# Nine head pairs alone instead of twelve, and one batch's first chunk beside the next three

## The chip, the cores and the metric

The kernel runs on one core of one Trainium2 chip. The metric is the device time of one launch in microseconds (us). Three runs of the kernel before gave 1332.28, 1333.82 and 1337.2 us, median 1333.82.

## What is computed

Attention over 4 batches, 12 heads, 448 positions and a head width of 64, with q and k normed by their root mean square, and then two dense layers without a residual:

```python
q_n, k_n = rmsnorm(q, g_q), rmsnorm(k, g_k)          # over the 64 of a head
attn = softmax(q_n @ k_n.T / 8);  x = attn @ v       # (4, 12, 448, 64)
x = x.transpose(0, 2, 1, 3).reshape(1792, 768)
h = x @ w_in;   x = (s * relu(h)**2 + b) @ w_out     # layer 1: 768 -> 2048 -> 768
h = x @ w2_in;  out = (h * cos(h)) @ w2_out          # layer 2, the same sizes
```

All is float32; the weights reach the device as 64-bit floats.

## The kernel before, in words

**Pairs.** Attention goes through 24 pairs of heads, six to a batch, numbered here 0 to 23 in that order; names in the trace carry batch and pair of the batch, so pair 8 is `1_2`. A pair is done in four chunks of 112 queries. A chunk is two score products on TensorE (PE, `sc`, line 193), two row maxima on VectorE (DVE, `top`, line 205), two exponentials on ScalarE (ACT, `pr`, line 208), and two chunks later eight transposes (`tp`, line 226) copied out by ACT and DVE (`pT`). Once a pair: squares (ACT, line 135), their sums (DVE, `ss`, line 141), the norms (ACT and GpSimd (POOL), lines 150 to 162), the transposes of q and k (`pt_q`, `pt_k`, line 173, copied out as `qT` and `kT`), the product with v (`av`, line 249) and its scaling (DVE, `xf`, line 257). The score product of a chunk also waits for the exponentials of two chunks earlier (line 197).

**Layers.** A layer's 2048 hidden columns go in 8 chunks of two column tiles. Each product is three passes of split operands (high by high, low by high, high by low). An *in* unit (line 400, 18 matmuls) makes one hidden tile for one batch, an *out* unit (line 452, or 479 in layer 2) adds a chunk to the result; in layer 1 an out unit is 6 matmuls.

**Weights.** A weight tile comes in two halves. A half of raw weight is a DMA, two ACT passes (lines 371, 372), three DVE passes (375 to 377), a store to DRAM in layer 1 (line 380), an ACT cast (338) and a subtraction on POOL (339). A half that was stored before is a DMA, the cast and a subtraction on DVE. Three weight tiles are held.

**Order.** All pairs of batches 0 and 1 (12) run alone. Then layer 1 of these two batches runs, chunk after chunk, beside the 12 pairs of batches 2 and 3, whose results go to DRAM. They are reloaded (`reload`, line 512; `xr`, then the split `xh` and `xl`) for layer 1 of batches 2 and 3, and layer 2 follows for all four. The units stand in one list; after each unit, `steps` is drawn on as far as a cost account allows (line 588), and a scheduler then sets the order on each engine from readiness. `ALONE` counts the batches whose pairs run alone and take their PSUM banks for `pt`, `rt` and `av` from the pool that the layers use later (line 165); other pairs take them from the two `tp` banks. The first six raw halves are held back behind chosen exponentials (line 374), the first weight DMA behind the score product of step `START` (line 364).

Of the kernel before, what the change touches and what calls it, by code (L numbers as in the profile page):

```python
# [33 lines left out]
def body(ctx, tc, q, k, v, g_q, g_k, w1_in, w1_out, s_in, b_in, w2_in, w2_out, out):  # L34
    nc = tc.nc
    B, H, S, D = q.shape
# [3 lines left out]
    NCH = 4  # L40
# [8 lines left out]
    NT = 2 * S // P  # L49
    SKEW = 2  # L50
    LAG_T = 2
    START, GATE = 10, 33
    ALONE = 2
    PAIR = 12.1
    LOOK = 8

# [54 lines left out]
    def attention(keep):  # L111
# [3 lines left out]
        tail = {}  # L115

        def line(engine, first, last=None):
            if engine in tail and (engine == "PE" or len(exps) <= NCH * NP * ALONE):
                issue_after(first, tail[engine])
            tail[engine] = last or first  # L120
            return first
# [40 lines left out]
                    rs[:, n].unsqueeze(3).to_broadcast([CP, 2, NCH, D]), ALU.mult)  # L162

        def bank(i, name):
            if pairs[i][0] < ALONE:
                return psm.tile([P, 512], F32, tag="mo", name=name, bufs=2)
            return ps.tile([P, 512], F32, tag="tp", name=name)

# [93 lines left out]
        def emit(f, i, *a):  # L262
            if 0 <= i < len(pairs):
                f(i, *a)
# [13 lines left out]
        squares(1)  # L278
        means(1)
        norms(1)  # L280
        for s in range(n + 5):
            i, r = divmod(s, NCH)
            old = i - 1 if 0 < i <= len(pairs) else None
            alone = old is not None and pairs[old][0] < ALONE
            cost = 0.0
            if r == 1:
                emit(load, i, "v")
                emit(load, i + 3, "qk")
                emit(flip, i + 1, "q")
                cost += 0.46  # L290
            if r == 2:
                emit(flip, i + 1, "k")
                cost += 0.46
            if s < n:
                scores(s)
                cost += 0.93
            if r == 1:
                emit(unflip, i + 1, "q")
            if r == 2:
                emit(unflip, i + 1, "k")  # L300
            if r == 3 and old is not None and not alone:
                finish(old)
            if LAG_T <= s < n + LAG_T:
                turn(s - LAG_T)
                cost += 0.9
            if r == 0:
                if 0 <= i - 2 < len(pairs) and pairs[i - 2][0] < ALONE:
# [12 lines left out]
            if i == 0 and r < 3:  # L320
                for part in ((), (squares,), (means, norms))[r]:
                    emit(part, 2)
            else:
                if r == 0:
                    emit(means, i + 2)
                if r == 1:
                    emit(norms, i + 2)
                if r == 3:
                    emit(squares, i + 3)
            yield cost  # L330


# [8 lines left out]
    def load_weight(key):  # L341
        layer, seg, kind, a, e = key
        w = ((w1_in, w1_out), (w2_in, w2_out))[layer][kind]
        name = "_".join(map(str, key))
        wh = wp.tile([P, 2 * CW], F32R, tag="wh", name=f"wh_{name}", bufs=3)
        wl = wp.tile([P, 2 * CW], F32R, tag="wl", name=f"wl_{name}", bufs=3)
        weights[key] = wh, wl
        for o in range(2):
            kk = f"{name}_{o}"
            hi_part, lo_part = (z[:, o * CW:(o + 1) * CW] for z in (wh, wl))  # L350
            if (layer, kind, a, e, o) in plain:
                t = wp.tile([P, CW], F32, tag="t", name=f"t_{kk}", bufs=3)
                nc.sync.dma_start(t, plain[layer, kind, a, e, o])
                halves(t, hi_part, lo_part, nc.vector)
                continue
            own = "xb" in pools or count["raw"] % 3 < 2
            raw = (wp if own else pools["att"]).tile([P, CW], I64, tag="raw", name=f"raw_{kk}", bufs=2 if own else 1)
            count["raw"] += 1
            if kind == 0:
                src = w[o * CW:(o + 1) * CW, a * P:(a + 1) * P].rearrange("(c p) f -> p c f", p=P)  # L360
                dma = nc.sync.dma_start(raw.rearrange("p (c f) -> p c f", f=P), src)
            else:
                dma = nc.sync.dma_start(raw, w[(CF * a + o) * P:(CF * a + o + 1) * P, e * CW:(e + 1) * CW])
            if seg == 0 and kind == 0 and a == 0:
                follow(dma, marks["start"])
            ru = raw.bitcast(U32).rearrange("p (n two) -> p n two", two=2)
            lo, hi = ru[:, :, 0], ru[:, :, 1]
            c = wp.tile([P, CW], U32, tag="c", name=f"c_{kk}", bufs=2)
            cf = c.bitcast(F32)
            t = wp.tile([P, CW], U32, tag="t", name=f"t_{kk}", bufs=3)  # L370
            for z in (nc.scalar.activation(cf, hi.bitcast(F32), AF.Copy, scale=2.0**-112),  # L371
                      nc.scalar.activation(t, lo, AF.Copy, scale=LSCALE, bias=-0.5)):
                if count["raw"] <= 6:
                    issue_after(z, exps[GATE + 2 * (count["raw"] - 1)])
            nc.vector.scalar_tensor_tensor(t, hi, 0x80000000, t, ALU.bitwise_and, ALU.bitwise_or)  # L375
            nc.vector.tensor_scalar(cf, cf, VMAX, -VMAX, ALU.min, ALU.max)
# [137 lines left out]
        nc.sync.dma_start(t, stash[layer, b, c])  # L514
        xs.setdefault((layer, b), []).append(split(t, pool, f"{layer + 1}_{b}_{c}", nc.vector if c % 4 < 2 else nc.gpsimd))

    segs = [(0, (0, 1), range(NCK)), (0, (2, 3), range(NCK)), (1, (0, 1, 2, 3), range(NCK))]
    units = []
    chunks = [(seg, ck) for seg, (_, _, r) in enumerate(segs) for ck in r]
    ins = [[("in", segs[seg][0], seg, ck, f, b) for f in range(CF) for b in segs[seg][1]] for seg, ck in chunks]  # L520
# [1 line left out]
    for seg, ck in chunks:  # L522
# [6 lines left out]
    for n in range(len(chunks)):  # L529
        if chunks[n][0] < 2 and chunks[n + 1][0] != chunks[n][0]:  # L530
            ins[n].sort(key=lambda u: (u[5], u[4]))
    for n, (seg, ck) in enumerate(chunks):
        units += ins[n][SKEW if n else 0:]
        if n + 1 < len(chunks):
            if chunks[n + 1][0] != seg:
                units.append(("next", seg + 1))
            early = ins[n + 1][:SKEW]
        else:
            early = []
        units += early + outs[n]  # L540

    def weight_of(u):
        kind, layer, seg, ck, a, b = u
# [16 lines left out]
        while finished["pairs"] < batches * NP:  # L560
            next(steps)

    until(ALONE)
    last = {max(n for n, u in enumerate(units) if u[:3] == ("in", 0, 0) and u[5] == b): b + ALONE for b in range(ALONE)}
    rate = 1.05 * PAIR * NP * (B - ALONE) / sum(3.39 if u[0] == "in" else 1.13 for u in units[:min(last)])
    debt = 0.0
    seg = 0
    again = []
    for n, u in enumerate(units):
        ahead(n + LOOK)  # L570
        if u[0] == "next":
            seg = u[1]
            if seg == 1:
                for _ in steps:
                    pass
                att_scope.close()
                pools["xb"] = ctx.enter_context(tc.tile_pool(name="xb", bufs=2 * NE))
                pools["mb"] = ctx.enter_context(tc.tile_pool(name="mb", bufs=2))
                pools["psb"] = ctx.enter_context(tc.tile_pool(name="psb", bufs=2, space=PSUM))
                again = [(1, b, c, pools["xb"]) for b in range(2) for c in range(NE)]  # L580
            continue
        if seg == 1 and again and n % 4 == 0:
            reload(*again.pop(0))
        if seg > 1:
            while again:
                reload(*again.pop(0))
        for cost in (unit_in if u[0] == "in" else unit_out)(*u[1:]):
            debt += cost * rate
            while debt > 0:
                c = next(steps, None)  # L590
                if c is None:
                    break
                debt -= c
        if n in last:
            until(last[n] + 1)
            for c in range(NP):
                reload(0, last[n], c, xa)


_INS = ['q', 'k', 'v', 'g_q', 'g_k', 'moe_w_in', 'moe_w_out', 'moe_s', 'moe_b', 'moe2_w_in', 'moe2_w_out']  # L600
# [25 lines left out]
```

## Time and profile before

| | |
|---|---|
| median of three runs | 1333.82 us |
| the profiled execution, its span | 1332.04 us, 1330.3 us |
| mean granted clock of TensorE | 0.986 |
| PE, DVE, ACT, POOL busy | 95%, 63%, 56%, 42% of the span |
| HBM traffic | 82 GB/s |

Stages, by what PE does: pairs alone to 204 us, layer 1 of batches 0 and 1 beside pairs 12 to 23 to about 546 us, layer 1 alone to about 850 us, layer 2 to the end. Busy PE is not PE at its peak: matmuls overlap, so one that is busy for 0.37 us follows the one before after about 0.20 us.

### The profile page before, as it was taken

Reading aid. Unit: us, or ns where it says so; the run is one execution under the profiler, and the core shown is the slowest. Engines: PE = TensorE matmul, PEld = TensorE weight load, DVE = VectorE, ACT = ScalarE, POOL = GpSimd, SP = SyncE. Lnnn points to the kernel's source line nnn. Section 1 sums busy time; section 2 is a strip of 40 time slices with the busy share of each in tenths; the row PEclk is TensorE's granted clock in tenths of the full one; section 3 lists DMA queues with packets and bytes.
Section 4 is the critical chain, followed back from the end, with each engine's and each line's share of the span. In section 5 each row is a group of like instructions: output and inputs, shape, how many; then the busy total and the mean of one; then the engine's idle time right before and its main releaser. Section 6 shows DMA issues by size and latency. Waiting matters only on the chain.

```text
span 1330.3 us, 18663 instructions
## 1 busy us (share of the span) xinstructions
PE 1261.0 (95%) x6624; PEld 1041.2 (78%) x6624; DVE 837.6 (63%) x1444; ACT 750.2 (56%) x1686; POOL 563.5 (42%) x624
## 2 busy tenths in 40 slices
PE   5999889999998999989999999989999999999998
PEld 2444437676776776878999999879999999999997
DVE  5666855568667676565444445754667677666655
ACT  5777856665555555444522223587756666566641
POOL 2334536453543423444422223454635544444531
PEclk9999979999999999999999999989999999999999
DMA  3212522433433333345311112211112122111105
GB/s 95 79 50 60 153 87 87 133 100 110 125 100 109 99 115 98 101 146 188 101 56 60 48 57 69 69 51 48 48 48 57 56 63 65 48 48 49 48 13 166
DMA packets 80382, 109.75 MB, mean 83 GB/s; under 512 B 7072, under 2 KB 70304, under 8 KB 80288
## 3 DMA queue, kind: packets, MB, share of 16 engines
q1 hardware_dynamic: 80288, 108.56, 27.4%
q8 instruction: 52, 0.85, 0.3%
q14 instruction: 42, 0.34, 0.1%
HBM read 84.94 MB, written 23.59 MB: 82 GB/s over the span
## 4 chain that ended last, share of the span: by engine, by line
PE 60%; DVE 14%; ACT 10%; DMA 7%; POOL 5%; issue 4%; SPq 0%; ACTq 0%; POOLq 0%; DVEq 0%
PE ph L400 23%; PE po L479 15%; PE po L452 12%; PE av L249 4%; PE sc L193 3%; ACT pr L208 3%; DMA raw<-in_moe_w_in_dram 3%; DVE t L375 3%; DMA raw<-in_moe_w_out_dram 3%; DVE top L205 2%; PE tp L226 2%; DVE ss L141 2%; ACT c L371 1%; DVE gt L415 1%; POOL wl L339 1%
## 5 line engine op out<-in xcount | busy, mean ns | idle before, releaser
L400 PE MATMUL ph<-xh,wh 128*128 128x448 f32 x768 | 281.2, 371 | 5.0 <-ACT hs L418 4.3
L400 PE MATMUL ph<-xl,wh 128*128 128x448 f32 x768 | 282.9, 369 | 0.9 <-POOL xl L98 0.5
L400 PE MATMUL ph<-xh,wl 128*128 128x448 f32 x768 | 283.4, 370 | 0.2 <-DVE wl L339 0.2
L430 POOL TENSOR_TENSOR gl<-gt,gh 128x448 fp32r<-128x448 f32 x128 | 156.1, 1225 | 177.8 <-ACT gh L429 177.6
L339 POOL TENSOR_TENSOR wl<-t,wh 128x384 fp32r<-128x384 f32 x128 | 138.0, 1097 | 98.8 <-ACT wh L338 80.7
L208 ACT ACTIVATE pr<-sc,top 112x448 f32<-112x448 f32 x192 | 120.5, 631 | 84.9 <-DVE top L205 84.8
L400 PEld LDWEIGHTS ph<-xh,wh 128*128 128x128 f32 x768 | 145.0, 189 | 19.8 <-ACT hs L418 5.0
L452 PE MATMUL po<-gh,wh 128*128 128x448 f32 x384 | 146.6, 383 | 12.3 <-DVE acc L461 7.2
L400 PEld LDWEIGHTS ph<-xl,wh 128*128 128x128 f32 x768 | 144.9, 189 | 15.2 <-issue 2.7
L400 PEld LDWEIGHTS ph<-xh,wl 128*128 128x128 f32 x768 | 145.1, 189 | 12.8 <-issue 2.0
L479 PE MATMUL po<-wh,gh 128*128 128x384 f32 x448 | 151.1, 338 | 2.7 <-DVE acc L487 1.5
L479 PE MATMUL po<-wh,gl 128*128 128x384 f32 x448 | 149.8, 334 | 0.0
L479 PE MATMUL po<-wl,gh 128*128 128x384 f32 x448 | 149.1, 334 | 0.0
L205 DVE TENSOR_REDUCE top<-sc 112x1 f32<-112x448 f32 x192 | 112.1, 618 | 57.1 <-PE sc L193 57.0
L461 DVE TENSOR_TENSOR acc<-po,acc 128x448 f32<-128x448 f32 x168 | 102.5, 619 | 69.2 <-PE po L452 68.7
L226 PEld LDWEIGHTS tp<-ident,pr 112*112 112x112 f32 x768 | 79.6, 136 | 82.3 <-DVE pT L230 21.5
L452 PE MATMUL po<-gh,wl 128*128 128x448 f32 x384 | 142.5, 371 | 1.1 <-POOL wl L339 1.1
L452 PE MATMUL po<-gl,wh 128*128 128x448 f32 x384 | 142.1, 371 | 0.0
L371 ACT ACTIVATE c<-raw 128x384 f32<-128x384 f32 x128 | 71.2, 556 | 119.8 <-DMA raw<-in_moe_w_out_dram 50.3
L487 DVE TENSOR_TENSOR acc<-po,acc 128x384 f32<-128x384 f32 x196 | 105.4, 551 | 50.7 <-PE po L479 50.5
L338 ACT CAST wh<-t 128x384 fp32r<-128x384 f32 x192 | 90.4, 512 | 83.0 <-PE po L452 45.3
L428 POOL TENSOR_TENSOR gt<-hs,gt 128x448 f32<-128x448 f32 x64 | 78.5, 1227 | 122.0 <-ACT gt L427 116.8
(82 smaller groups left out, 2241.4 us busy)
## 6 DMA issues: line engine op xcount, KB each, us to landing
raw<-in_moe_w_in_dram SPq DMA_DIRECT2D x64, 384.0 KB, 3.6
raw<-in_moe_w_out_dram SPq DMA_DIRECT2D x64, 384.0 KB, 3.4
wd<-t SPq DMA_DIRECT2D x64, 192.0 KB, 3.8
t<-wd SPq DMA_DIRECT2D x64, 192.0 KB, 2.4
rawq<-in_q_dram SPq DMA_DIRECT2D x24, 224.0 KB, 2.6
rawk<-in_k_dram SPq DMA_DIRECT2D x24, 224.0 KB, 3.0
rawv<-in_v_dram SPq DMA_DIRECT2D x24, 224.0 KB, 3.2
xd<-xf SPq DMA_DIRECT2D x12, 224.0 KB, 3.4
```

The lines of the kernel that those rows point to most:

```text
L205: line("DVE", nc.vector.tensor_reduce(tops[j], sc[j], axis=AX.X, op=ALU.max, negate=True))
L208: e = line("ACT", nc.scalar.activation(pr, sc[j], AF.Exp, bias=tops[j], scale=1.0, accum_out=st[i]["sums"][:, c, j:j + 1]))
L226: mm = [nc.tensor.transpose(tp[:, kc * CP:(kc + 1) * CP], pr[:, kc * CP:(kc + 1) * CP], ident[:CP, :CP]) for kc in range(NCH)]
L338: nc.scalar.copy(wh, w)
L339: eng.tensor_tensor(wl, w, wh.bitcast(F32), ALU.subtract)
L371: for z in (nc.scalar.activation(cf, hi.bitcast(F32), AF.Copy, scale=2.0**-112), nc.scalar.activation(t, lo, AF.Copy, scale=LSCALE, bias=- ...
L400: nc.tensor.matmul(h, a, m, start=(c == 0 and n == 0), stop=(c == NE - 1 and n == 2))
L430: nc.gpsimd.tensor_tensor(gl, gt, gh.bitcast(F32), ALU.subtract)
L452: marks["out"] = nc.tensor.matmul(po, a, m, start=(f == 0 and n == 0), stop=(f == CF - 1 and n == 2))
L461: nc.vector.tensor_tensor(at, po, at, ALU.add)
L479: nc.tensor.matmul(po, a, m, start=(f == 0 and n == 0), stop=(f == CF - 1 and n == 2))
L487: nc.vector.tensor_tensor(at, po, at, ALU.add)
```

## The change

- `ALONE` becomes a count of pairs, 9. Pairs 9 to 23 take the `tp` banks.
- Layer 1 gets five segments in place of two: chunk 0 for batch 0 alone, chunks 1 to 7 for batches 0 and 1, chunk 0 for batch 1 alone, then batches 2 and 3. The weights of chunk 0 are therefore loaded once more: 4 tiles, 8 stored halves.
- Segment 0 stands beside pairs 9 to 11, chunks 1 to 7 beside pairs 12 to 23, each with a rate of its own. Before chunk 1 the pairs of batch 1 are drawn to their end.
- `START` is 5 instead of 10; the six held raw halves wait for every fourth exponential from 12 on instead of every second from 33 on.
- The squares of a pair are emitted at step 2, their sums at step 3, the norms at the next step 0 (before: 3, next 0, next 1). The load of q and k comes after the sums.
- Reloads go out one after each unit, not six at once. The first in units of the next segment are sorted by batch; at the change to layer 2, four in units for batches 0 and 1 stand between the last twelve out units, three after each.

```diff
-    START, GATE = 10, 33
-    ALONE = 2
+    START, GATE = 5, 12
+    ALONE = 9
...
         def bank(i, name):
-            if pairs[i][0] < ALONE:
+            if i < ALONE:
                 return psm.tile([P, 512], F32, tag="mo", name=name, bufs=2)
...
+        load(3, "qk")
         for s in range(n + 5):
...
-                emit(load, i + 3, "qk")
...
-            else:
-                if r == 0:
-                    emit(means, i + 2)
-                if r == 1:
-                    emit(norms, i + 2)
-                if r == 3:
-                    emit(squares, i + 3)
...
+            if r == 0 and i > 0:
+                emit(norms, i + 2)
+            if r == 2:
+                emit(squares, i + 3)
+            if r == 3:
+                emit(means, i + 3)
+                emit(load, i + 4, "qk")
...
-                    issue_after(z, exps[GATE + 2 * (count["raw"] - 1)])
+                    issue_after(z, exps[GATE + 4 * (count["raw"] - 1)])
...
-    segs = [(0, (0, 1), range(NCK)), (0, (2, 3), range(NCK)), (1, (0, 1, 2, 3), range(NCK))]
+    segs = [(0, (0,), [0]), (0, (0, 1), range(1, NCK)), (0, (1,), [0]), (0, (2, 3), range(NCK)), (1, (0, 1, 2, 3), range(NCK))]
+    L2 = 4
...
+        ins[n + 1].sort(key=lambda u: (u[5] // 2, u[4], u[5]) if u[1] else (u[5], u[4]))
...
+            if given == 4:
+                for z in range(4):
+                    units += [ins[n + 1][z]] + outs[n][3 * z:3 * z + 3]
+            elif given:
+                units += ins[n + 1][:given] + outs[n]
...
-    rate = 1.05 * PAIR * NP * (B - ALONE) / sum(3.39 if u[0] == "in" else 1.13 for u in units[:min(last)])
+    rates = [1.05 * PAIR * (2 * NP - ALONE) / spent(units[:enter[0]]), 1.05 * PAIR * 2 * NP / spent(units[enter[0]:min(last)])]
...
             if seg == 1:
+                until(2)
+            if seg == 3:
                 for _ in steps:
                     pass
...
+        if soon:
+            reload(*soon.pop(0))
...
             until(last[n] + 1)
-            for c in range(NP):
-                reload(0, last[n], c, xa)
+            soon += [(0, last[n], c, xa) for c in range(NP)]
```

**DVE while pairs run alone.** Before, from the third chunk of pair 2 on; the pair that runs next is 3, and `ss_0_5` are the sums for pair 5:

```order
L205 TENSOR_REDUCE top_0_2_0_431<-sc_0_2_3_1_547 112x1
L230 COPY pT_0_2_1_534<-tp_0_2_1_1_562 112x4x112
L205 TENSOR_REDUCE top_0_3_0_588<-sc_0_3_0_0_583 112x1
L205 TENSOR_REDUCE top_0_3_0_588<-sc_0_3_0_1_584 112x1
L230 COPY pT_0_2_1_534<-tp_0_2_2_1_601 112x4x112
L257 TENSOR_TENSOR xf_0_1_573<-av_0_1_541,xf_0_1_573 128x448
L214 RECIPROCAL sums_0_2_0_430<-sums_0_2_0_430 112x8
L141 TENSOR_REDUCE ss_0_5_616<-nq_0_5_579 112x8
L141 TENSOR_REDUCE ss_0_5_616<-nk_0_5_581 112x8
L205 TENSOR_REDUCE top_0_3_0_588<-sc_0_3_1_0_632 112x1
```

The same place in the changed kernel, where `c_0_0_0_0_0_0` and `t_0_0_0_0_0_0` belong to the first raw weight half:

```order
L205 TENSOR_REDUCE top_0_2_0_440<-sc_0_2_3_1_551 112x1
L230 COPY pT_0_2_1_534<-tp_0_2_1_1_566 112x4x112
L141 TENSOR_REDUCE ss_0_5_583<-nq_0_5_546 112x8
L141 TENSOR_REDUCE ss_0_5_583<-nk_0_5_548 112x8
L205 TENSOR_REDUCE top_0_3_0_597<-sc_0_3_0_0_592 112x1
L205 TENSOR_REDUCE top_0_3_0_597<-sc_0_3_0_1_593 112x1
L230 COPY pT_0_2_1_534<-tp_0_2_2_1_610 112x4x112
L257 TENSOR_TENSOR xf_0_1_577<-av_0_1_541,xf_0_1_577 128x448
L214 RECIPROCAL sums_0_2_0_439<-sums_0_2_0_439 112x8
L205 TENSOR_REDUCE top_0_3_0_597<-sc_0_3_1_0_643 112x1
L376 TENSOR_SCALAR c_0_0_0_0_0_0_1739<-c_0_0_0_0_0_0_1739 128x384
L205 TENSOR_REDUCE top_0_3_0_597<-sc_0_3_1_1_644 112x1
```

The two sums moved from ahead of chunk 1's maxima to ahead of chunk 0's, and a weight half's passes now stand around chunk 1's second maximum.

**ACT, the first weight halves that are not held back.** Before, ahead of the exponentials of pair 11's first chunk (`pr_1_5_0`):

```order
L371 ACTIVATE c_0_0_0_2_0_1_2264<-raw_0_0_0_2_0_1_2262 128x384
L372 ACTIVATE t_0_0_0_2_0_1_2265<-raw_0_0_0_2_0_1_2262 128x384
L371 ACTIVATE c_0_0_1_0_0_0_2279<-raw_0_0_1_0_0_0_2277 128x384
L372 ACTIVATE t_0_0_1_0_0_0_2280<-raw_0_0_1_0_0_0_2277 128x384
L240 COPY xf_1_3_1829<-rt_1_3_1824 128x448
L135 ACTIVATE nq_2_1_1835<-rawq_2_1_1722 112x512
L135 ACTIVATE nk_2_1_1837<-rawk_2_1_1724 112x512
L372 ACTIVATE t_0_0_1_0_0_1_2293<-raw_0_0_1_0_0_1_2290 128x384
L338 CAST wh_0_0_0_2_0_2247<-t_0_0_0_2_0_1_2265 128x384
L371 ACTIVATE c_0_0_1_0_0_1_2292<-raw_0_0_1_0_0_1_2290 128x384
L208 ACTIVATE pr_1_5_0_0_1847,sums_1_5_0_1843<-sc_1_5_0_0_1839,top_1_5_0_1844 112x448
```

Now, ahead of those of pair 8's second chunk (`pr_1_2_1`):

```order
L371 ACTIVATE c_0_0_1_0_0_1_1808<-raw_0_0_1_0_0_1_1806 128x384
L372 ACTIVATE t_0_0_1_0_0_1_1809<-raw_0_0_1_0_0_1_1806 128x384
L371 ACTIVATE c_0_0_1_0_1_0_1823<-raw_0_0_1_0_1_0_1821 128x384
L372 ACTIVATE t_0_0_1_0_1_0_1824<-raw_0_0_1_0_1_0_1821 128x384
L372 ACTIVATE t_0_0_1_0_1_1_1837<-raw_0_0_1_0_1_1_1834 128x384
L97 CAST xh_1_1_0_1402<-xf_1_0_1362 128x448
L152 ACTIVATE y_1_4_1412<-ln_1_4_1410 112x16
L208 ACTIVATE pr_1_2_1_0_1434,sums_1_2_0_1381<-sc_1_2_1_0_1428,top_1_2_0_1382 112x448
```

The cluster of weight passes stands three pairs earlier, and the squares no longer stand in it.

**PE where layer 1 begins.** Before, its first matmul stands after the score products of pair 13's first chunk (`sc_2_1_0`):

```order
L193 MATMUL sc_2_1_0_0_2153<-kT_2_1_2095,qT_2_1_2055 112x448
L193 MATMUL sc_2_1_0_1_2154<-kT_2_1_2095,qT_2_1_2055 112x448
L226 MATMUL tp_2_0_2_0_2165<-ident_73,pr_2_0_2_0_2091 112x112 x4
L226 MATMUL tp_2_0_2_1_2171<-ident_73,pr_2_0_2_1_2093 112x112 x4
L400 MATMUL ph_0_0_0_2303<-xh_1_0_0_451,wh_0_0_0_0_0_2191 128x448
```

Now it stands after those of pair 10's (`sc_1_4_0`):

```order
L193 MATMUL sc_1_4_0_0_1691<-kT_1_4_1624,qT_1_4_1595 112x448
L193 MATMUL sc_1_4_0_1_1692<-kT_1_4_1624,qT_1_4_1595 112x448
L226 MATMUL tp_1_3_2_0_1703<-ident_73,pr_1_3_2_0_1620 112x112 x4
L226 MATMUL tp_1_3_2_1_1709<-ident_73,pr_1_3_2_1_1622 112x112 x4
L400 MATMUL ph_0_0_0_1847<-xh_1_0_0_460,wh_0_0_0_0_0_1735 128x448
```

So layer 1 begins exactly three pairs earlier in PE's order.

## Rows read from the trace of the kernel before

**Rows 1.** The page, first part: PE's busy time, share, instructions.

```profile
PE 1261.0 (95%) x6624; PEld 1041.2 (78%) x6624; DVE 837.6 (63%) x1444; ACT 750.2 (56%) x1686; POOL 563.5 (42%) x624
```

**Rows 2.** Stretches: from:to length, busy by engine (instructions), granted clock, DMA.

```profile
34.40:114.80 80.40, 72.86 (x458) 37.67 (x457) 54.35 (x103) 57.92 (x163) 30.25 (x61) 1.00 0.21 62
156.00:204.00 48.00, 39.37 (x197) 18.73 (x196) 30.79 (x61) 31.41 (x85) 21.89 (x38) 0.82 0.38 110
204.00:546.00 342.00, 325.95 (x1753) 240.50 (x1753) 230.69 (x413) 200.74 (x487) 148.74 (x181) 0.99 0.35 106
546.00:612.00 66.00, 61.47 (x285) 53.27 (x282) 37.53 (x63) 27.31 (x54) 29.68 (x28) 0.97 0.49 149
612.00:850.00 238.00, 237.22 (x1168) 218.81 (x1167) 124.32 (x208) 88.50 (x179) 82.30 (x76) 1.00 0.24 74
850.00:890.00 40.00, 34.42 (x154) 30.22 (x153) 27.20 (x39) 26.35 (x55) 21.09 (x17) 0.91 0.24 69
```

**Rows 3.** PE's timeline, one pair alone: start, length, instruction, [idle before, what ended it].

```profile
101.41 1.72 PE L249 MATMUL av<-pT,rawv 112*64 112x448 f32 x8
...
113.11 0.59 PE L226 MATMUL tp<-ident,pr 112*112 112x112 f32 x4 [0.69 <-DVE pT L230]
114.28 0.59 PE L226 MATMUL tp<-ident,pr 112*112 112x112 f32 x4 [0.57 <-ACT pT L232]
114.80 1.72 PE L249 MATMUL av<-pT,rawv 112*64 112x448 f32 x8
```

**Rows 4.** DVE's timeline in the same pair.

```profile
107.99 1.16 DVE L205 TENSOR_REDUCE top<-sc 112x1 f32<-112x448 f32 x2 [2.20 <-PE sc L193]
...
110.12 0.19 DVE L214 RECIPROCAL sums<-sums 112x8 f32<-112x8 f32 x1
110.23 0.64 DVE L141 TENSOR_REDUCE ss<-nq 112x8 f32<-112x512 f32 x1
110.78 0.68 DVE L141 TENSOR_REDUCE ss<-nk 112x8 f32<-112x512 f32 x1
111.38 1.15 DVE L205 TENSOR_REDUCE top<-sc 112x1 f32<-112x448 f32 x2
```

**Rows 5.** ACT's timeline in the same pair.

```profile
110.29 0.58 ACT L97 CAST xh<-xf 128x448 fp32r<-128x448 f32 x1
112.03 0.63 ACT L208 ACTIVATE pr<-sc,top 112x448 f32<-112x448 f32 x1 [1.16 <-DVE top L205]
```

**Rows 6.** PE's timeline from pair 9's `av` to the first matmul of layer 1.

```profile
156.05 1.72 PE L249 MATMUL av<-pT,rawv 112*64 112x448 f32 x8
...
166.08 0.85 PE L173 MATMUL pt_q<-ident,nq 112*128 112x112 f32 x4 [2.56 <-DVE pT L230]
...
172.05 0.60 PE L226 MATMUL tp<-ident,pr 112*112 112x112 f32 x4 [2.43 <-ACT qT L182]
...
177.74 3.26 PE L249 MATMUL av<-pT,rawv 112*64 112x448 f32 x8
...
204.05 0.45 PE L400 MATMUL ph<-xh,wh 128*128 128x448 f32 x1
```

**Rows 7.** Groups of weight passes, DVE in 34 to 160 us.

```profile
L375 DVE SCALAR_TENSOR_TENSOR t<-raw,t 128x384 uint32<-128x384 uint32 x5 | 2.8, 553 | 0.2
```

**Rows 8.** Groups of weight passes, DVE and ACT in 204 to 546 us.

```profile
L375 DVE SCALAR_TENSOR_TENSOR t<-raw,t 128x384 uint32<-128x384 uint32 x49 | 35.2, 722 | 20.5 <-ACT t L372 20.4
...
L371 ACT ACTIVATE c<-raw 128x384 f32<-128x384 f32 x48 | 26.8, 557 | 43.3 <-DVE t L377 19.5 <-DMA raw<-in_moe_w_in_dram 13.5 <-DMA raw<-in_moe_w_out_dram 9.1
```

**Rows 9.** PE's waits in 546 to 612 us: total, times, longest.

```profile
PE po L452 <- ACT wh L338: 1.4, 1, 1.4
PE po L452 <- POOL wl L339: 1.1, 1, 1.1
```

**Rows 10.** PE's waits in 850 to 890 us.

```profile
PE ph L400 <- ACT hs L418: 4.3, 2, 2.9
```

More of the change, by code (lines that the diff above doesn't have):

```diff
@@ L117, in line @@
         def line(engine, first, last=None):
-            if engine in tail and (engine == "PE" or len(exps) <= NCH * NP * ALONE):
+            if engine in tail and (engine == "PE" or len(exps) <= NCH * ALONE):
                 issue_after(first, tail[engine])
@@ L283, in attention @@
             old = i - 1 if 0 < i <= len(pairs) else None
-            alone = old is not None and pairs[old][0] < ALONE
+            alone = old is not None and old < ALONE
             cost = 0.0
@@ L306, in attention @@
             if r == 0:
-                if 0 <= i - 2 < len(pairs) and pairs[i - 2][0] < ALONE:
+                if 0 <= i - 2 < ALONE:
                     finish(i - 2)
@@ L319, in attention @@
                 mix(old, range(2, NCH))
-            if i == 0 and r < 3:
-                for part in ((), (squares,), (means, norms))[r]:
-                    emit(part, 2)
-            else:
-                if r == 0:
-                    emit(means, i + 2)
-                if r == 1:
-                    emit(norms, i + 2)
-                if r == 3:
-                    emit(squares, i + 3)
+            if i == 0 and r in (1, 2):
+                for part in ((squares,), (means, norms))[r - 1]:
+                    part(2)
+            if r == 0 and i > 0:
[5 more added lines that the diff above has]
+                emit(load, i + 4, "qk")
             yield cost
@@ L528, in body @@
             outs.append([("out", 1, seg, ck, eh, t) for t in range(2 * NT) for eh in range(2)])
-    for n in range(len(chunks)):
-        if chunks[n][0] < 2 and chunks[n + 1][0] != chunks[n][0]:
+    edge = [n for n in range(len(chunks) - 1) if chunks[n + 1][0] != chunks[n][0]]
+    for n in edge:
+        if segs[chunks[n][0]][0] == 0:
             ins[n].sort(key=lambda u: (u[5], u[4]))
+        ins[n + 1].sort(key=lambda u: (u[5] // 2, u[4], u[5]) if u[1] else (u[5], u[4]))
+    given = 0
     for n, (seg, ck) in enumerate(chunks):
[L533 to L537, printed above, removed]
-        else:
-            early = []
-        units += early + outs[n]
+        units += ins[n][given:]
+        given = 0
+        if n in edge:
+            if chunks[n + 1][0] == 2:
+                given = SKEW
+            if chunks[n + 1][0] == L2:
+                given = 4
+            if given != SKEW:
+                units += outs[n] if not given else []
+            units.append(("next", seg + 1))
+            if given == 4:
[3 more added lines that the diff above has]
+                units += ins[n + 1][:given] + outs[n]
+        else:
+            given = SKEW if n + 1 < len(chunks) else 0
+            units += (ins[n + 1][:given] if given else []) + outs[n]
     def weight_of(u):
@@ L561, in until, with spent @@
             next(steps)
-    until(ALONE)
-    last = {max(n for n, u in enumerate(units) if u[:3] == ("in", 0, 0) and u[5] == b): b + ALONE for b in range(ALONE)}
-    rate = 1.05 * PAIR * NP * (B - ALONE) / sum(3.39 if u[0] == "in" else 1.13 for u in units[:min(last)])
+    def spent(part):
+        return sum(3.39 if u[0] == "in" else 1.13 for u in part if u[0] != "next")
+    while finished["pairs"] < ALONE:
+        next(steps)
+    enter = [units.index(("next", seg)) for seg in range(1, L2 + 1)]
+    last = {max(n for n, u in enumerate(units) if u[:3] == ("in", 0, 1 + b) and u[5] == b): b + 2 for b in range(2)}
+    rates = [1.05 * PAIR * (2 * NP - ALONE) / spent(units[:enter[0]]), 1.05 * PAIR * 2 * NP / spent(units[enter[0]:min(last)])]
     debt = 0.0
     seg = 0
-    again = []
+    soon, again = [], []
     for n, u in enumerate(units):
@@ L581, in body @@
             continue
-        if seg == 1 and again and n % 4 == 0:
+        if soon:
+            reload(*soon.pop(0))
+        elif again and n % 4 == 0:
             reload(*again.pop(0))
-        if seg > 1:
-            while again:
+        if u[0] == "in":
+            while soon and len(xs.get((u[1], u[5]), [])) < NE:
+                reload(*soon.pop(0))
+            while again and u[1] == 1:
                 reload(*again.pop(0))
         for cost in (unit_in if u[0] == "in" else unit_out)(*u[1:]):
-            debt += cost * rate
+            debt += cost * rates[min(seg, 1)]
             while debt > 0:
```

## The prediction

> **What bounds the kernel now.** I read the page's busy shares first, then the stretches of the span, then the timelines of PE, DVE and ACT in one clean pair, then PE's timeline ahead of layer 1, and last PE's waits at the two changes of batch and layer. The reader is to see PE busy for 95% of the span [rows 1], so that a gain can come only from PE's idle and slow time, and is to see where that lies.
>
> Six pairs alone take 80.40 us, 13.40 each; PE is busy for 72.86 / 6 = 12.14 us of it, ACT for 57.92 / 6 = 9.65, DVE for 54.35 / 6 = 9.06 [rows 2]. A pair alone is a chain that passes PE, DVE and ACT in turn, and PE idles for 1.26 us in it, in two gaps [rows 3]. From 156 to 204 us it goes worse: PE is busy for 39.37 of 48 us at a mean clock of 0.82 [rows 2]. With pairs beside layer 1, to 546 us, PE idles for 342 - 325.95 = 16.05 us, 4.7%. Layer 1 alone leaves PE nothing to give: 237.22 us for 1168 matmuls are 0.203 us each, in 238 us. The two changes, 546 to 612 and 850 to 890 us, idle 4.53 and 5.58 us, with clocks of 0.97 and 0.91 [rows 2].
>
> **The change part by part.** The sum is made against the profiled execution's own 1332.04 us, 1.78 below the median.
>
> *Sums of squares.* In a clean pair DVE is free after the reciprocal at 110.23 us, but two `ss` come first, and the maxima of chunk 1 start at 111.38, 1.15 us late [rows 4]. ACT idles for 1.16 us for them [rows 5], and PE's two gaps of 0.69 and 0.57 us follow from that [rows 3]. Ahead of chunk 0's maxima DVE idles for 2.20 us [rows 4], and that is where the change puts the `ss`: they are hidden there. A clean pair should take 13.40 - 1.15 = 12.25 us, near PE's 12.14. But the first six raw halves now start at pair 3 instead of pair 8, one a pair. Between chunk 0's copy and chunk 1's exponentials ACT then has two weight passes, about 2 x 0.56 us by the row for the first [rows 8], which fills the 1.16 us that came free. So only the pairs without a half gain, 1 and 2: 2 x 1.15 = 2.3 us; pairs 3 to 7 I put at 13.2, 0.2 less each, 1.0. Pair 6's `av`, at 114.80 us [rows 3], comes at 111.5. Bounds: none of the 3.3, if the start is late by as much, or 7 x 1.15 = 8.
>
> *The crowded pairs.* From pair 9's `av` at 156.05 to the first matmul of layer 1 at 204.05 us are 48.0 us [rows 6], for ten chunks, 2.5 pairs, which at 13.40 us would take 33.5; weight passes in them add some 2. In the order of instructions the same cluster of weight passes stands three pairs earlier, now in pair 8, with as many passes on ACT and DVE. Before, PE waited for 2.56 us for DVE's copy and for 2.43 us for ACT's [rows 6]; from then on its instructions take twice their time (`av` 3.26 us against 1.72), the lower of its two clocks, 1.2 GHz for 2.4. The squares leave the cluster, and after it the pairs lack the late `ss`. I take 43 us for the stretch, nearer to the 48.0 measured than to the 36 that would be left without the stall; bounds 36 and 52. The first matmul of layer 1 then comes at 111.5 + 43 = 154.5 us.
>
> On this the Trainium skill speaks against the change: its page "TensorE: Matmul & The Clock Gate" (HAM oscillation — how this bites in real kernels) says that an array left waiting loses its clock and begins the next piece of work slow, again at each wait. The trace agrees with it here, at 0.82. By that rule the cluster keeps its full price and 48 us stand where I put 43, 5 us more in the sum.
>
> *Three pairs beside one batch's chunk.* PE then has pairs 9 to 11, 3 x 12.14 = 36.4 us, and 72 matmuls (2 in units of 18, 6 out units of 6), 14.6 us at 0.203: 51.0 us. ACT has 3 x 9.65 = 29.0 us for the pairs, 8 raw halves of chunk 1 of three passes at some 0.56 us [rows 8], 13.4, and ten passes for the units, 5.6: 48 of 51 us, 94%, where the mixed stage so far has 200.74 of 342, 59% [rows 2]. No stretch of before is mixed so tightly; the nearest rows are the mixed stage, 4.7% idle or 2.5 us, and the crowded pairs, 18% idle or 11 us. In this stretch the in units of batch 1 for chunk 1 wait for pair 11's split; behind them in PE's order stand pairs already drawn, about one of them alone, with its 1.26 us of gaps. I take 6 in all, so 57 us, to 211.5. Before, the same work stood done at 204.05 + 14.6 x 1.047 = 219.3 us. Gain 7.8 us, the two parts above included.
>
> The Trainium skill, "GPSIMD Engine Reference" (Specifications), says that POOL shares SBUF access with DVE and slows DVE instructions with two SBUF operands. The trace agrees: line 375 takes 0.553 us alone [rows 7] and 0.722 us in the mixed stage [rows 8]. By that, 8 halves moved here would cost DVE 16 x 0.17 = 2.7 us; DVE has room for them, so the sum stays.
>
> *Chunks 1 to 7.* Twelve pairs stand beside 7 chunks instead of 8, at the same idle share a little more crowded; flips of pairs 9 to 11 share the two `tp` banks. Cost 2 us, between 0 and 5.
>
> *Change of batches.* PE waits for 1.4 us for a weight cast and 1.1 for a weight's low part [rows 9], idles for 4.53 in all, and a clock of 0.97 over 66 us costs some 2 more. Between batch 0's last in unit and batch 2's first there will be 2 in and 6 out units more, 14.6 us, so the reloads are hidden. Each is a DMA on SP's queue, a cast on ACT and a subtraction on DVE or POOL; SP works in order, and a reload that waits for one of its two buffers holds the weight DMAs behind it, which is less likely at one a unit than at six at once. But the four tiles that come again are each used for half as long, 3.7 us, with three held. Gain 2.5 us; bounds a loss of 5 and a gain of 6.
>
> *Change of layer.* PE waits for 4.3 us for ACT's `hs` [rows 10], idles for 5.58 and has a clock of 0.91 over 40 us. Four in units spread over twelve out units give ACT room there; the same ACT passes come a little earlier, no fewer. Gain 3 us; bounds a loss of 4 and a gain of 8.
>
> *At nothing:* 8 stored halves more (a DMA, a cast, a DVE pass each) beside PE work; an earlier `START`, whose DMAs land long before use; their queue, SP, has room at a DMA share of 0.21 [rows 2].
>
> Sum: -7.8 + 2 - 2.5 - 3 = -11.3 us: 1320.7 by the profiled execution, 1322.5 by the median. I predict 1322 us.
>
> **The rivals.** *The stall comes along unchanged and ACT sets the dense stretch.* The cluster has the same passes, and ACT at 94% cannot absorb waits. First matmul at 159.5, stretch 51 + 10: 220.5 against 219.3; the rest nets -2: 1331 to 1333 us, no change. Against it: squares and sums leave the crowded place.
>
> *The slow clock follows into the dense stretch (slower).* Before, the first stretch of layer 1 after the stall had full PE work and the clock came back. Now PE meets a stretch that ACT limits. The crowded ten chunks did 2.5 x 12.14 = 30.4 us of PE's work in 48.0, 0.63 of it. At that pace PE's 51 us take 81 us, 24 more than in my sum: 1346 us. It decides from about 76 us for the stretch on, which gives 1341. For it: the clock of 0.82 [rows 2]; against: from 204 to 546 us the clock was 0.99.
>
> *The stall goes away.* Without the squares the cluster fits, PE never waits for over 2 us, the clock stays up: 36 us instead of 43, and the dense stretch at 4.7% instead of 6 us: 1322 - 7 - 3.5 = 1311 us, and as little as 1304 with both changes at their upper bounds.
>
> *The change doesn't reach the layer change.* PE's `hs` wait comes from ACT's total there, and stays: 1325 us.
>
> **How the numbers follow.** My forecast, with the last rival inside it (1316 to 1327): 0.42. The stall goes away (1304 to 1316): 0.23. Unchanged (1327 to 1340): 0.22. Slower: 0.13. The range 1307 to 1338 leaves out the far ends of the first and last cases. 0.5%, about what a measurement of this kernel can tell from no change, is 6.7 us: faster is below 1327.1, slower above 1340.5. Faster: 0.42 + 0.23 less a little of the forecast's upper end, 0.64; same 0.24; slower 0.12.
>
> **What the new profile would show.** Clean early pairs with `av` to `av` of 12.2 to 12.4 us and no gap at the two `tp` of chunk 2; from pair 3 on 13.2. The first `ph` near 154 us; a clock near 0.9 ahead of it. PE idle for some 6 us in the 57 us after. In the change of batches no wait for `xh` or `xl`; at the change of layer fewer waits for `hs`. I am wrong in kind if the first `ph` comes after 165 us, if the stretch after it takes over 70 us, or if PE waits for a `wh` or `wl` of chunk 0's second load.

## The result and the profile after

The changed kernel takes 1316.5 us (median of four runs, 1311.2 to 1319.6) against 1335.3 for the kernel before (four runs): 0.986 of its time, with a 95% interval of 0.982 to 0.990. Predicted were 1322, in a range of 1307 to 1338. In the comparison below it took 1318.0 against 1332.5, 0.988 [0.986, 0.990].

The profiled execution took 1311.19 us, 20.8 less than the profiled one of before, and is the quickest of the four. Its granted clock was 0.996, that of the longest, 1319.6 us, 0.990: of 1318 us the difference of 0.006 is 7.9 us, about the whole spread. That is an estimate from the mean clocks alone, and the clock is not all that varies: five more runs of the same kernel, told below, spread over 5.3 us at clocks of 0.990 to 0.992. So a median is compared with a median here, and the traces are read for places.

The page, first part, as [rows 1]:

```profile
PE 1246.8 (95%) x6624; PEld 1033.3 (79%) x6624; DVE 845.8 (65%) x1452; ACT 755.4 (58%) x1694; POOL 569.6 (43%) x624
```

The stretches of the changed kernel, to set against [rows 2]: six pairs alone, the crowded pairs up to the first `ph`, the dense stretch, pairs 14 to 23, the change of batches, the change of layer (columns as there).

```profile
33.90:112.60 78.70, 72.76 (x457) 37.68 (x456) 62.28 (x117) 63.07 (x178) 34.91 (x63) 1.00 0.31 90
112.60:156.30 43.70, 35.23 (x198) 16.89 (x197) 31.15 (x60) 30.52 (x82) 20.50 (x35) 0.92 0.39 116
156.30:217.60 61.30, 57.71 (x331) 41.52 (x328) 39.03 (x73) 43.48 (x111) 30.54 (x38) 1.00 0.34 103
...
304.20:558.40 254.20, 245.59 (x1340) 182.42 (x1339) 181.40 (x319) 145.38 (x349) 108.16 (x128) 0.99 0.35 108
558.40:603.80 45.40, 42.49 (x205) 35.86 (x204) 26.22 (x44) 15.26 (x31) 13.21 (x13) 1.00 0.55 171
...
840.00:890.00 50.00, 46.26 (x231) 41.34 (x230) 29.67 (x42) 40.77 (x88) 30.12 (x25) 1.00 0.17 48
```

The reader is to see that the crowded pairs are still there, at a mean clock of 0.92, and that the stretches behind them run at 0.99 or 1.00.

DVE between the first `av` of pair 2 and that of pair 3, to set against [rows 4]: the two `ss` stand where DVE would wait for scores, and 1.02 us are still free ahead of the next maxima.

```profile
63.32 0.61 DVE L230 COPY pT<-tp 112x448 f32<-112x448 f32 x1
63.85 0.67 DVE L141 TENSOR_REDUCE ss<-nq 112x8 f32<-112x512 f32 x1
64.45 0.67 DVE L141 TENSOR_REDUCE ss<-nk 112x8 f32<-112x512 f32 x1
66.14 1.15 DVE L205 TENSOR_REDUCE top<-sc 112x1 f32<-112x448 f32 x2 [1.02 <-PE sc L193]
```

PE in the crowded pairs, to set against [rows 6]:

```profile
121.03 0.57 PE L173 MATMUL pt_q<-ident,nq 112*128 112x112 f32 x4 [0.95 <-DVE pT L230]
...
126.23 0.59 PE L226 MATMUL tp<-ident,pr 112*112 112x112 f32 x4 [3.16 <-ACT qT L182]
...
132.53 0.57 PE L226 MATMUL tp<-ident,pr 112*112 112x112 f32 x4 [2.21 <-DVE kT L184]
133.03 2.63 PE L249 MATMUL av<-pT,rawv 112*64 112x448 f32 x8
...
156.28 0.45 PE L400 MATMUL ph<-xh,wh 128*128 128x448 f32 x1
```

The same three waits as before stand here, at the same three instructions. Of those before, [rows 6] show the first two; the third is

```profile
176.85 0.96 PE L226 MATMUL tp<-ident,pr 112*112 112x112 f32 x4 [1.00 <-DVE kT L184]
```

To compare kernels of different order place by place, the next table gives the time of a pair's first `av` less 0.2027 us (the distance of two starts in layer 1 alone) for each matmul of layer 1 issued ahead of it; the last row also takes off 0.172 us for each out matmul of layer 2. What is left grows by the pairs' own time and by every loss. The kernels named are those of the experiments; split_only's trace is of the longest of its twelve executions, 1338.9 us. The last row of the second execution and of split_only holds some 5 us of the slower pace that the last section tells of.

| us | before | after, two executions | sums_only | split_only | no_split | spread9 | flips_mo |
|---|---|---|---|---|---|---|---|
| `av` of pair 6 | 114.8 | 112.6, 112.3 | 107.3 | 122.0 | 109.8 | 110.8 | 110.5 |
| first `ph`, as it stands | 204.1 | 156.3, 156.0 | 190.3 | 169.5 | 192.7 | 153.2 | 143.4 |
| pair 14 | 237.1 | 233.7, 234.4 | 225.2 | 249.1 | 225.4 | 232.0 | 222.3 |
| pair 23 | 360.8 | 348.2, 351.0 | 350.4 | 367.1 | 350.2 | 349.5 | 337.8 |
| chunk 1 of batches 2, 3 | 372.3 | 355.5, 360.7 | 362.5 | 374.9 | 361.4 | 356.7 | 345.0 |
| chunk 3 of layer 2 | 384.7 | 362.6, 371.5 | 374.9 | 391.1 | 368.7 | 363.2 | 351.6 |

### The profile page after: what moved, and what is told of

Same layout as the page of the kernel before. It is cut to its first block, busy times and chain, and to the rows that moved or that the text cites. A ratio compares the mean times of both kernels' runs of the same rounds, so it can differ in the third digit from the quotient of the medians.

```text
span 1309.4 us, 18684 instructions
## 1 busy us (share of the span) xinstructions
PE 1246.8 (95%) x6624; PEld 1033.3 (79%) x6624; DVE 845.8 (65%) x1452; ACT 755.4 (58%) x1694; POOL 569.6 (43%) x624
## 4 chain that ended last, share of the span: by engine, by line
PE 67%; ACT 11%; DVE 10%; DMA 5%; POOL 3%; issue 3%; SPq 0%; ACTq 0%; DVEq 0%; POOLq 0%
PE ph L400 26%; PE po L479 14%; PE po L452 13%; PE av L249 5%; PE sc L193 4%; PE tp L226 3%; ACT pr L208 3%; DMA raw<-in_moe_w_out_dram 2%; DVE t L375 2%; DVE top L205 2%; DMA xr<-xd 1%; DMA raw<-in_moe_w_in_dram 1%; DVE gt L425 1%; ACT c L371 1%; ACT pT L232 1%
## 5 line engine op out<-in xcount | busy, mean ns | idle before, releaser
L430 POOL TENSOR_TENSOR gl<-gt,gh 128x448 fp32r<-128x448 f32 x128 | 158.9, 1246 | 184.4 <-ACT gh L429 184.3
L338 ACT CAST wh<-t 128x384 fp32r<-128x384 f32 x200 | 94.6, 512 | 85.9 <-PE po L452 47.9
```

Of the source, the lines that this page charges most:

```text
L338: nc.scalar.copy(wh, w)
L430: nc.gpsimd.tensor_tensor(gl, gt, gh.bitcast(F32), ALU.subtract)
```

## The experiments

Times are medians; beside each stands the ratio to the kernel before with its interval.

**after_again**: the changed kernel, unedited.

> The changed kernel once more, unchanged. The theory of the prediction (the gain is made of less waiting: the early start and the dense stretch 8 us, the two changes of batch and layer together 6 or more): median 1313 to 1319 us, and in the new trace the first ph again near 156 us and the change of batches without a wait for a weight. The rival (most of the gain of the profiled execution is chance in the clock: 14 us at half clock there, 37 us in the one of before): the stretches at half clock come back in another place and number, and the stages from 212 to 545 us lose what they gained.

1318.0 us (0.988 [0.986, 0.990]). The first `ph` came at 155.97 us, and the change of batches had no wait for a weight; waits came back to a tenth of a microsecond (an `rt` waits for 1.91 and for 1.90 us near 302 us). What such a wait does to the clock did not: of the matmuls close behind that one, all but the first are 0.37 us long in the first execution, and two are 0.57 us in the second. Over the 5 us from 303, from 416 and from 467 us the second execution has a clock of 0.66 each time, and reload_once and rate_100, in which PE has the same order, have 0.66 or less there; the first execution has 1.00 at all three, and 0.66 over the 5 us from 362 us instead. Both theories have a part. The places of the waits are lasting; some 5 of the profiled 20.8 us were luck (1311.2 us against the median of 1316.5).

**sums_old**: the places of squares, sums, norms and loads undone.

```diff
...
-            if r == 2:
-                emit(squares, i + 3)
-            if r == 3:
-                emit(means, i + 3)
-                emit(load, i + 4, "qk")
...
+                if r == 0:
+                    emit(means, i + 2)
+                if r == 1:
+                    emit(norms, i + 2)
+                if r == 3:
+                    emit(squares, i + 3)
```

> The changed kernel with squares, sums, norms and loads of q and k in their old places, all else as changed. By the prediction the re-placing is worth 3 us in the early pairs and a part of the 5 us in the crowded pairs: 1320 to 1325 us, a clean pair of 13.4 us, pair 6's av at 115 us, the first ph at 160 to 165. Rival one, the sums are only hidden work: 1316 us, the first ph at 156. Rival two, the sums are most of the gain, in the mixed stage too: 1328 us or more.

1322.95 us (0.993 [0.990, 0.995]), pair 6's `av` at 118.2 us, the first `ph` at 163.9. The time is as forecast, and the re-placing is worth 5 us here; pair 6's `av` came 3 us later than expected.

**sums_only**: the same edit the other way round, on the kernel before.

> The kernel before with only the squares, sums, norms and loads in their new places. By the prediction each clean pair gives 1.15 us, here seven of them (8 us), and the stall before layer 1 a part of its 5 us: 1323 to 1329 us with the first ph at 190 to 198 in place of 204. Rival one (nothing without the earlier start): 1332 to 1337 us. Rival two (sums are most of the gain, all stages): 1316 to 1320 us, no start of layer 1 is needed to be earlier.

1323.1 us (0.992 [0.990, 0.994]): 9.4 us from this edit alone, almost twice what it gives inside the change. With twelve pairs alone and the halves held late, seven pairs carry no weight half and come 12.36 us apart; in the changed kernel only one such step is left.

**layer_old**: the order at the change to layer 2 undone.

```diff
...
-            if chunks[n + 1][0] == 2:
+            if chunks[n + 1][0] in (2, L2):
                 given = SKEW
-            if chunks[n + 1][0] == L2:
-                given = 4
...
-            if given == 4:
-                for z in range(4):
-                    units += [ins[n + 1][z]] + outs[n][3 * z:3 * z + 3]
-            elif given:
+            if given:
```

> The changed kernel with the change to layer 2 as before: two in units ahead of the last twelve out units in their old order, not four among them. By the prediction the new order is worth 3 us (bounds a loss of 4, a gain of 8): 1319 to 1320 us, with a wait of PE for hs of over 2 us again between 840 and 890 us and a clock below 0.95 there. Rival (ACT's total at the change sets it): 1316 to 1317 us, the same waits in both.

1321.6 us (0.991 [0.989, 0.993]): 3.6 us, as predicted. PE's waits from 830 to 895 us (total, times, longest), first of the changed kernel:

```profile
PE ph L400 <- ACT hs L418: 2.2, 3, 1.1
PE po L479 <- ACT acc L485: 1.4, 2, 0.8
```

and of the one with the old order, where the waits of [rows 10] are back, and the clock is 0.93 from 840 to 890 us in place of 1.00:

```profile
PE ph L400 <- ACT hs L418: 4.3, 2, 3.0
PE po L479 <- ACT gh L429: 1.0, 1, 1.0
```

**no_split**: sums_only with the new order at the change of layer; twelve pairs alone, chunk 0 not split.

> The kernel before with the squares, sums, norms and loads in their new places and the new order at the change to layer 2, but with twelve pairs alone, one segment for batches 0 and 1, and six reloads at once. If the parts simply add (9.4 us for the sums, 3.6 for the change of layer): 1319 to 1320 us, so that nine pairs alone, the split of chunk 0 and the spaced reloads together are worth 1.5 us. By the prediction (early start and dense stretch 8 us with the sums, change of batches 2.5) they are worth 5 to 6: 1323 to 1324 us. In either case pairs 14 to 23 idle for 13 to 14 us on PE and the change of batches loses 11 to 12 us, as in both kernels with the old segments.

1316.5 us (0.988 [0.986, 0.990]), the time of the changed kernel to within 1.5 us. Nine pairs alone, the split and the spaced reloads brought nothing on top of the other two parts.

**split_only**: the changed kernel with both other parts undone (the diffs of sums_old and layer_old).

> The changed kernel with both the squares, sums, norms and loads in their old places and the old order at the change to layer 2, so that of the change only the earlier start, the split of chunk 0 and the spaced reloads are left. With both others and without these, the kernel took 1316.5 us, the same as with all; if the parts added, these would be worth nothing alone: 1330 to 1333 us. If they and the sums gain by the same thing (sums are worth 9 us alone, 5 on top of the split): 1325 to 1328 us.

1329.8 us (0.998 [0.997, 1.000], twelve runs): almost nothing alone either, so the parts nearly add. The table shows where, for its longest execution: its early pairs are worse (pair 6 at 122.0 us, where they carry weight halves on top of the late `ss`), 12 us are lost by pair 14, and half of that comes back by pair 23.

**reload_once**: six reloads in a row.

```diff
-            soon += [(0, last[n], c, xa) for c in range(NP)]
+            for c in range(NP):
+                reload(0, last[n], c, xa)
```

> The changed kernel with the six reloads of a batch issued at once instead of one after each unit. The stretch from pair 23's av to the second chunk of batches 2 and 3, less layer work, costs 7 to 10 us in the changed kernel, 11 to 12 with the old segments. If the spacing of the reloads makes that difference: 1320 to 1322 us and waits for wh and wl, or for xh and xl, near 570 to 600 us. If the eight units of batch 1's chunk 0 make it, which hide the reloads: 1317 to 1319 us and no such waits.

1313.3 us (0.987 [0.984, 0.989]): not slower, so the spacing is not what helps. PE's waits in the change of batches, of this kernel (560 to 606 us):

```profile
PE po L452 <- DVE acc L461: 3.0, 3, 1.3
```

and of no_split (533 to 610 us), where those of [rows 9] stand again:

```profile
PE po L452 <- ACT wh L338: 1.4, 1, 1.4
...
PE po L452 <- POOL wl L339: 1.1, 1, 1.1
```

With the split and nine pairs alone no wait for a weight over 0.2 us stands there in any trace, and the table gives some 4 us for it (2 in the second execution). But late_split, below, has both waits again, at 535 us, so eight more units are not enough by themselves.

**rate_100**: the pairs beside chunks 1 to 7 drawn 5% slower.

```diff
-    rates = [..., 1.05 * PAIR * 2 * NP / spent(units[enter[0]:min(last)])]
+    rates = [..., 1.00 * PAIR * 2 * NP / spent(units[enter[0]:min(last)])]
```

> The changed kernel with the pairs of batches 2 and 3 drawn 5% slower beside chunks 1 to 7 (a factor of 1.00 for 1.05), which moves every pair against the units. If the mixed stage's gain over before (PE idles for 8.4 us in pairs 14 to 23, 13.6 with the old segments) is made by where single steps meet single units: idle time changes by several us either way, and the time with it, 1314 to 1324 us. If it comes from the structure (seven chunks, not eight, and their weights ahead): idle stays at 8 to 9 us and the time at 1317 to 1319 us.

1315.3 us (0.987 [0.985, 0.989]), PE idle for 8.2 us in pairs 14 to 23. But the edit did not reach PE: by line and name its 6624 operations have the same order as in the changed kernel, and pair 23's first `av` stands behind 1037 matmuls of layer 1 in both. So the run decides nothing between the two theories. In all nine kernels with the split PE idles for 7.4 to 8.6 us from pair 14 to pair 23, in all four without it for 13.1 to 14.0. Up to pair 23 eight of the nine have one and the same order on PE (late_split has its own) and the four another, so these are three orders, not thirteen. That window, of sums_only:

```profile
274.70:532.90 258.20, 244.16 (x1307) 179.34 (x1306) 183.59 (x327) 145.15 (x352) 107.46 (x128) 0.97 0.36 110
```

and of split_only, 14.0 us idle against 8.2:

```profile
319.90:577.50 257.60, 249.44 (x1340) 185.09 (x1339) 179.05 (x317) 145.32 (x349) 107.86 (x128) 0.98 0.35 106
```

So the gain goes with the new list of units. Whether its structure makes it, or one meeting of a step with a unit, and which, stays open.

**spread9**: nine weight halves held back, closer together.

```diff
-    START, GATE = 5, 12
+    START, GATE = 5, 8
...
-                if count["raw"] <= 6:
-                    issue_after(z, exps[GATE + 4 * (count["raw"] - 1)])
+                if count["raw"] <= 9:
+                    issue_after(z, exps[GATE + 3 * (count["raw"] - 1)])
```

> The changed kernel with nine raw halves held back instead of six, every third exponential from the eighth on instead of every fourth from the twelfth, so that the passes of three more halves no longer stand in a row at pair 8. Theory: at pairs 6 to 8 ACT stands in line with weight passes that wait for buffers (1.74 and 0.71 us in the trace), the copies for PE come late and the clock falls: 20.4 and 16.0 us for two pairs that should take 13.3. Without the cluster some 7 to 10 us go, and three halves more in the early pairs cost 0.9 us each: 1311 to 1314 us, first ph at 149 to 152. Rival (the work of the passes itself fills these pairs, wherever it stands): 1317 to 1319 us, first ph at 154 to 157.

1311.2 us (0.984 [0.981, 0.986]), in the theory's range, but the first `ph` came at 153.2, between the two, and pair 6 to pair 8 still took 35.2 us (36.4 in the changed kernel). The three waits of the crowded pairs stayed with the cluster of passes taken apart:

```profile
119.20 0.57 PE L173 MATMUL pt_q<-ident,nq 112*128 112x112 f32 x4 [0.95 <-DVE pT L230]
...
123.87 0.99 PE L226 MATMUL tp<-ident,pr 112*112 112x112 f32 x4 [2.63 <-ACT qT L182]
...
129.30 0.97 PE L226 MATMUL tp<-ident,pr 112*112 112x112 f32 x4 [1.00 <-DVE kT L184]
```

So the cluster is a small part. The first row is what these share with the changed kernel and with [rows 6]: a `pt_q`, and in the order of each it is that of the first pair that is not alone.

**no_split_spread** (`START, GATE = 10, 14` and the same hold, on no_split) and **late_split** (the changed kernel with this hold, `ALONE = 12` and one rate).

> The kernel with twelve pairs alone, the squares and sums in their new places and the new order at the change to layer 2 (1316.5 us), with nine raw halves held back instead of six, every third exponential from the fourteenth on. If the cluster at the last pairs alone costs here what it cost in the changed kernel (6 us): 1309 to 1312 us, as fast as the changed kernel with the same hold (1311.2), and the earlier start is then worth nothing with or without the cluster. Rival (earlier start pays once the cluster is gone): 1314 to 1317 us.

> The same again, with the changed kernel's segments (chunk 0 for one batch first, for batch 1 before the change of batches) and spaced reloads, but twelve pairs alone, all of layer 1's first part beside pairs 12 to 23 at one rate. The split gave 4 us at the change of batches in all traces; what it lost lay in the three pairs beside one batch's chunk, which stand alone here. If that holds: 1305 to 1308 us, the fastest, with 7 to 8 us lost from pair 23's av to the second chunk of batches 2 and 3. Rival (the mixed stage gives it back, fewer pairs beside the same units): 1309 to 1313 us.

1314.3 us (0.986 [0.985, 0.988]) and 1312.4 (0.985 [0.982, 0.988]), both in the rivals' ranges. The hold gives 2 us with twelve pairs alone, less than the 6 with nine. Late_split's six runs spread from 1304.8 to 1320.3 us, too far to tell it from the others. From pair 23's `av` to the second chunk of batches 2 and 3 it lost 15 us by the reckoning of the table, twice the 7 to 8 expected, with the two waits for a weight and a clock of 0.91 from 521.6 to 560 us.

**flips_mo**: spread9, with the transposes of q and k of pairs 9 and 10 in the banks of the pairs alone.

```diff
-        def bank(i, name):
-            if i < ALONE:
+        def bank(i, name, more=0):
+            if i < ALONE + more:
...
-            pt = bank(i, f"pt_{nm}_{b}_{hp}")[:, :S]
+            pt = bank(i, f"pt_{nm}_{b}_{hp}", 2)[:, :S]
```

> The kernel with nine halves held back (1311.2 us), in which the transposes of q and k of the first two pairs that are not alone, 9 and 10, take their banks from the pool of the pairs alone and not from the two tp banks. Theory: the crowded pairs are made by the banks and not by the weight passes. In all kernels the stall begins at the first pt_q that takes a tp bank (121 us in the changed kernel, 166 us before): pt_q waits for a copy of pT, the next tp for the copy of qT, the one after for kT. With other banks these waits go: 12.3 to 13.5 us for each of the pairs 6 to 8 in place of 19.4 and 15.8, first ph at 144 to 147 us, and 1302 to 1305 us. Rival (the weight passes, or the chunks' chain itself, keep ACT and DVE late there): first ph at 152 to 154, 1309 to 1313 us.

1301.3 us (0.976 [0.973, 0.979]; 1299.6 to 1303.4), the fastest of all, 10 us below spread9. The three waits are gone, and the first `ph` comes at 143.4 us; PE's timeline:

```profile
117.78 0.55 PE L173 MATMUL pt_q<-ident,nq 112*128 112x112 f32 x4
120.01 0.55 PE L173 MATMUL pt_k<-ident,nk 112*128 112x112 f32 x4
122.30 0.60 PE L226 MATMUL tp<-ident,pr 112*112 112x112 f32 x4 [0.80 <-DVE pT L230]
123.65 0.59 PE L226 MATMUL tp<-ident,pr 112*112 112x112 f32 x4 [0.75 <-ACT pT L232]
...
143.36 0.45 PE L400 MATMUL ph<-xh,wh 128*128 128x448 f32 x1
```

and the stretch from pair 6's `av` to the first `ph`, first of spread9, then of this kernel:

```profile
110.78:153.23 42.45, 35.73 (x197) 17.59 (x197) 28.38 (x53) 27.72 (x75) 16.48 (x32) 0.88 0.29 85
110.50:143.36 32.86, 31.27 (x197) 15.96 (x197) 28.00 (x53) 26.93 (x75) 16.17 (x31) 1.00 0.33 102
```

These 9.6 us are nearly all of the gain: PE idles for 5.1 us less, and for the same 197 matmuls it is busy for 4.5 us less, at the higher clock.

A `tp` does not read `qT`. It waits for `qT`'s copy because `pt_q` sits in one of the two `tp` banks until ACT has read it, and ACT has exponentials and weight passes ahead of that: in the changed kernel `pt_q` is done at 121.6 us, and ACT begins to read it at 125.63, behind five weight passes and two exponentials. Pairs alone keep their flips (the transposes of q and k) in other banks; later pairs have matmuls of a layer beside them, and between the first `ph` and 560 us no `tp` waits for `qT` or `kT` in the changed kernel's trace. Only the first two pairs after `ALONE` have neither.

The Trainium skill, "TensorE: Matmul & The Clock Gate" (A second HAM failure mode: psum-queue depth-cycling), tells of short idle times at the turn of PSUM banks that take the clock down again and again. The trace agrees in part: 0.88 with the flips in the `tp` banks, 1.00 without. But the waits alone do not settle it. No_split_spread has the three waits as well (0.95, 1.98 and 1.40 us), late_split too (0.95, 1.98 and 1.00 us), and from pair 9's `av` to the first `ph` the one has a clock of 1.00, the other 0.88:

```profile
148.34:186.83 38.49, 32.02 (x197) 15.98 (x197) 23.94 (x45) 25.02 (x69) 15.75 (x32) 1.00 0.21 62
148.50:190.61 42.11, 36.04 (x198) 17.76 (x197) 23.94 (x45) 25.02 (x69) 15.76 (x32) 0.88 0.20 57
```

So the waits are made by the banks, and what they cost in clock differs from trace to trace. Moved flips without the new hold, or with twelve pairs alone, were not run: what the cluster of passes costs once the banks are free, and whether the earlier start then earns anything, stays open.

## Why the prediction came out right, and where it was wrong

The sum was right in size, and its largest cause was wrong.

- *Sums of squares:* right in kind, 2.2 us for 3.3. Pair 6's `av` came at 112.6 us (111.5 predicted): a pair without a half took 12.36 us (12.25), but there was one such step and not two, and those with a half took 13.27 (13.2). PE's gaps at the two `tp` did not quite go: 0.29 us is left in the pair without a half.
- *The crowded pairs:* right in size, 43.7 us for 43, at a clock of 0.92. Wrong in cause: the prediction named the cluster of weight passes and ACT's late copies. Spread9 took the cluster apart and the waits stayed; flips_mo moved the banks and they went. [Rows 6] held the hint: a `tp` that waits for `qT`, which it does not read, but which is copied out of one of its banks. The prediction had seen that flips share the `tp` banks, and priced it under chunks 1 to 7 alone.
- *Three pairs beside one batch's chunk:* right at its end. When pair 13's first scores were issued, at 222.6 us, 66 more matmuls had been done than the 72 counted on: 222.6 - 66 x 0.203 = 209.2 us for 211.5. ACT did not fill it: it was busy for 43.48 of 61.30 us, 71%, where 48 of 51 was predicted.
- *Chunks 1 to 7:* wrong in sign. A cost of 2 was predicted. Behind pair 13's first scores PE idled for 4.1 of 24.4 us, and by pair 14 only 3.4 us of lead were left; but pairs 14 to 23 then took 114.5 and 116.6 us against 123.7, a gain of 7 to 9, of which 5 are PE's shorter idle time (8 us for 13); the rest was not taken apart.
- *Change of batches:* a gain of 4.2 us in the profiled execution and 1.8 in the second (2.5 predicted).
- *Change of layer:* 3.6 us between medians (3 predicted).

What failed as a whole is the first term, a gain of 7.8 for the earlier start. It was reckoned against the kernel before, with the new places of the sums counted in. The part alone would have shown that the sums give 9.4 us without an earlier start, and that the start then costs 8.5 by pair 14 (225.2 to 233.7) and earns it back behind. So the rival in which the stall comes along unchanged was nearer in size to what the split does, 3 us alone and none on top of the other two parts, though its dense stretch of 61 us did not come: by the reckoning above it took 209.2 - 156.3 = 52.9. The gain came from the two smaller edits, which with twelve pairs alone gave 15.8 us (no_split). In that rival's sum the parts behind the dense stretch net -3.5 us, not -2; all together it is -2.3, so that its 1331 to 1333 us stands; the low end of the rival in which the stall goes away comes to 1303 us, not 1304.

That the slow clock would follow into the dense stretch fell at once: its clock is 1.00, and PE idles for 3.6 of 61.3 us.

## What to carry to other kernels

Where PE waits for a copy that its instruction does not read, ask whether it waits for a PSUM bank: look for what else lives in that pool, and where a pool's users change, price the first users, who have nothing beside them. The Trainium skill, "Perfetto Trace Analysis" (Matmuls), asks for groups that turn through different banks; here other banks for the flips of two pairs were worth 10 us, more than the earlier start, the split and the spaced reloads together. And price each part of a change alone and on top of the others: the new places of the sums gave 9.4 us alone and 5 on top of the rest.

## What the runs showed that was not expected

The same matmuls run at two paces under a full granted clock. In layer 1 alone starts stand 202.7 ns apart in most executions, but 206.7 ns in after_again, rate_100 and split_only, from the change of batches on. The window of 90 us, of the changed kernel's first execution:

```profile
610.00:700.00 90.00, 90.00 (x446) 83.42 (x445) 39.81 (x69) 36.91 (x75) 32.73 (x31) 1.00 0.26 79
```

and of after_again, with nine matmuls fewer, PE busy throughout and the same clock:

```profile
610.00:700.00 90.00, 90.00 (x437) 81.73 (x436) 40.02 (x69) 35.38 (x73) 32.80 (x31) 1.00 0.27 80
```

That is 2%, some 4 us over the stage. In sums_only the pace fell near 590 us and came back near 620. What sets it stays open.
